# Attention and expert routing on one core: transposes of logits and early rows at the end of their slot, router constants in front

## The chip, the cores and the metric

The kernel runs on one core of one Trainium2 chip. The metric is the device time of one execution in microseconds. Five engines work from queues of their own, each in order, and wait for one another by semaphores: TensorE (PE in the profile; PEld is its weight load), VectorE (DVE), ScalarE (ACT), GpSimd (POOL) and SyncE (SP, which only issues transfers here).

## What is computed

```python
scores = scale * np.matmul(q, k.transpose(0, 1, 3, 2))        # q, k, v: 8 x 8 x 576 x 64
thresh = np.max(scores, axis=-1, keepdims=True) - tau
scores = np.where(scores >= thresh, scores, -1000000000.0)
attn = softmax(scores)                                        # sum + 1e-09 below
x = (attn @ v).transpose(0, 2, 1, 3).reshape(4608, 512)
logits = x @ w_gate                                           # 8 experts
# tokens go to experts greedily, by descending logit, at most 576 to an expert
for e in range(8): out[assigned == e] = np.maximum(x[assigned == e] @ w1[e], 0.0) @ w2[e]
```

## The kernel before

There are two stages. The first, `attention`, computes attention and logits for all 8 batches; the second, `moe`, chooses the tokens of each expert in turn (the class `Router` does that) and computes the experts. The change is in the first stage and in the constants that `Router` needs later.

A *pair* is two heads of one batch; there are 32 pairs, four to a batch. The scores of a pair are nine *tiles* of 128 rows by 576 keys: tiles 0 to 7 belong to one head each, tile 8 holds the last 64 rows of both heads ("a tile of two halves"). The work is written out by hand as a pipeline of *slots*, two tiles to a slot, 18 slots to a batch. The order of the program is the order in each engine's queue. In slot `s_` the loop does the following:

- `score` (L69, PE) computes the scores of two tiles into two PSUM tiles named `sc`. There are two such buffers in all, so the next slot's first scores need the first of them back and its second scores the second.
- `left` (L98, PE) turns the leftover columns of older tiles. It uses free columns of the last `sc` tile, from column HS = 288 on, in the two slots out of nine where a tile 8 is turned and the two after them (`p8` in the code).
- `beside`: in the other slots, one *side unit* if there is one, which also puts its results into the free columns of the `sc` tiles. Its PE part is issued here, behind the scores; its eviction `ev()` later on.
- `flush` (ACT) evicts finished outputs. `trev` (L116, L118, ACT) evicts the transposes `tb` of the slot before.
- `mx` (L74, DVE) copies the scores to `z` and reduces each row to its extreme; a threshold `nb` follows on POOL (L75). `ex` (L86, ACT) is the exponential of `z`. `leftev` (L128 to L131, ACT) evicts the leftovers.
- `stt` (L90, DVE) masks and sums the exponentials of the slot before, with the threshold of the slot before.
- `columns` issues *value units* (L155 and L165, PE): attention times v, taken from the list `queue` by due slots. Other entries of that list are run as they are reached: the reciprocals of a batch's sums (L170, L171, DVE), `finish`, and once, in the first batch, `Router.consts`. `whole` issues the logits of a finished batch (L177, PE), one half a slot.
- `tr` (L98, PE) turns two tiles of exponentials into `tb`, which has one buffer.

`finish(b)` puts the side units of batch b into the list `side`. `lgt_unit` turns the logits of the batch (ten transposes from `lt`, eight for one batch, and four small matmuls by `dup`, L185) into the free columns of both `sc` tiles; ACT evicts them (L217, L188, L219) and POOL scales and adds them (L222 to L229). It goes to the front of the list and becomes ready when the second half of the logits is evicted (L179). For the first two batches there are also ten units `xt_early`: each turns a quarter of the batch's attention output rows (four transposes from `xt`), ACT evicts it (L240), POOL copies the reciprocals (L239), and every second unit sends rows to DRAM.

`Router.consts` (L429 in the profile, since a wrapper records DVE's instructions) makes the router's constants on DVE from a table `cst` in SBUF, and two iotas on POOL.

The free slots of a batch, those without `p8`, are ten out of 18. Seen by their value work they come in three kinds: one whose second tile is a tile of two halves, one with eight matmuls L155 of 320 columns behind it, and one right after a slot of leftovers.

Of the kernel before, what the change touches and what calls it, by code (L numbers as in the profile page):

```python
# [22 lines left out]
def attention(ctx, tc, qk, vl, tau, wgd, xrows, xts, Lg, nb_batches, ident, dup, R, after_first):  # L23
# [28 lines left out]
        LD[p]=t  # L52


    SC={}; NBI={}; TH={}; PB={}; DEN={}
# [4 lines left out]
    def score(t):  # L60

        p,i=divmod(t,9); kd=LD[p]
        sc=ps_s.tile([128,2,512],F32,name="sc"); SC[t]=sc
        if i<8: todo=((i%2,slice(0,128),slice(i//2*128,i//2*128+128)),)
        else: todo=((0,slice(0,64),slice(512,576)),(1,slice(64,128),slice(512,576)))
        for h,o,c in todo:
            for f in range(2):
                r=slice(64*f,64*f+64)
                T.matmul(sc[o,f,:HS], kd["q",h][r,c], kd["k",h][r,:],start=True,stop=True)  # L69
# [97 lines left out]
    RD={}  # L167
# [13 lines left out]
    def free(t): return SC[t][:,:,HS:]  # L181
    def both(b,ps):
        for r in range(2):
            g=slice(64*r,64*r+64)
            T.matmul(ps[:,r,0:4],dup[g],RD[b][g,:,4,:,0],start=True,stop=True)  # L185
# [13 lines left out]
    def lgt_mm(b,c0,c1,ps):  # L199
        for c in range(c0,c1):  # L200
            a=HEAD(b)+128*c if c<2 else 128*c-256 if c<4 else 192 if b%2 and b<nb_batches-1 else 256
            turn(ps[:,:,64*(c-c0):64*(c-c0)+64],LT[b][:,a:a+128])
    def lgt_in(ps,n): return ps[:,:,0:64*n].rearrange("p r (m k) -> p r m k",k=32)[:,:,:,0:16]
    def logits(b,c0,c1,ps,o):
# [3 lines left out]
            V.tensor_tensor(w[:,:,:,r].rearrange("p c j h e -> p (c j) h e"),lv[:,r].rearrange("p m (h e) -> p m h e",h=2),  # L208
                RD[b][:,r,c0:c1].rearrange("p c j h -> p (c j) h").unsqueeze(3).to_broadcast([128,2*n,2,8]),op=ALU.mult)
        V.tensor_reduce(Lg[:,o:o+n,:],w.rearrange("p c j r h e -> p c e (j r h)"),axis=AX.X,op=ALU.add)  # L210
    def lgt_unit(b,ta,tb):
        n=5 if b<nb_batches-2 else 4
        x,y=free(ta),free(tb)
        lgt_mm(b,0,2,x); lgt_mm(b,2,n,y); both(b,x[:,:,128:])
        def ev():
            w=wk.tile([128,320],F32,name="lw",bufs=1).rearrange("p (r c j h e) -> p r c j h e",r=2,c=5,j=2,h=2)
            A.activation(w[:,:,0:2].rearrange("p r c j h e -> p r (c j) (h e)"),lgt_in(x,2),AF.Copy)  # L217
            both_ev(b,x[:,:,128:],slice(0,128),A)
            A.activation(w[:,:,2:n].rearrange("p r c j h e -> p r (c j) (h e)"),lgt_in(y,n-2),AF.Copy)  # L219
            for r in range(2):  # L220
                v=w[:,r,0:n].rearrange("p c j h e -> p (c j h) e")
                G.tensor_tensor(v,v,RD[b][:,r,0:n].rearrange("p c j h -> p (c j h)").unsqueeze(2).to_broadcast([128,4*n,8]),op=ALU.mult)  # L222
            v=w[:,:,0:n]
            G.tensor_tensor(v[:,0],v[:,0],v[:,1],op=ALU.add)
            G.tensor_tensor(v[:,0,:,0],v[:,0,:,0],v[:,0,:,1],op=ALU.add)
            G.tensor_tensor(Lg[:,4*b:4*b+4,:],v[:,0,0:4,0,0],v[:,0,0:4,0,1],op=ALU.add)
            if n==5:
                r=slice(64*(b%2),64*(b%2)+64)
                G.tensor_tensor(Lg[r,28+b//2,:],w[r,0,4,0,0],w[r,0,4,0,1],op=ALU.add)  # L229
        return ev  # L230
    XR={}
    def xt_early(b,c,i,t):
        n=128 if c<4 else 64
        y=free(t)
        for j in range(2): turn(y[:n,:,64*j:64*j+64],XT[b][:,2*i+j,c*128:c*128+n])
        if i==0: XR[b,c]=wk.tile([128,XW],F32,name="xr",bufs=XRB)
        xr=XR[b,c]
        def ev():
            if i==0: G.tensor_scalar(xr[:n,512:XW].rearrange("p (r k) -> p r k",r=2),RD[b][:n,:,c].rearrange("p r j h -> p r (j h)"),1.0,0.0,op0=ALU.mult,op1=ALU.add)  # L239
            A.activation(xr[:n,256*i:256*i+256].rearrange("p (j r d) -> p r j d",j=2,r=2),y[:n,:,0:128].rearrange("p r (j d) -> p r j d",j=2),AF.Copy)  # L240
            if i: nc.sync.dma_start(xrows[b*S+c*128:b*S+c*128+n,:],xr[:n])
        return ev
    def xt_unit(b,c,k=1):
        ps=bank_v([128,4,128],k)
        n=128 if c<4 else 64
# [25 lines left out]
        if j==3: queue.append(("n",lambda: not later,False,lambda: finish(b),p))  # L271
    def finish(b):
        aux.extend([lambda: lg_unit(b,0),lambda: lg_unit(b,1)])
        side.insert(0,(lambda: have.get("lt")==b,lambda *t: lgt_unit(b,*t)))
        rows=[lambda k=1,c=c: xt_unit(b,c,k) for c in range(5)]
        if nb_batches-NDEF-NBO<=b<nb_batches-NDEF:
            nc.sync.dma_start(xts[b],XT[b]); late2.extend(rows)
        elif b<nb_batches-NDEF: side.extend([(lambda: True,lambda ta,tb,c=c,i=i: xt_early(b,c,i,tb)) for c in range(5) for i in range(2)])
        else: late.extend(rows)
    def flush():  # L280
        for k,g in later: g(); k[0]=True
# [151 lines left out]
class Router:  # L433
    def __init__(s,ctx,tc,cst,off,Lg):
        nc=tc.nc; s.nc=nc; s.tc=tc
        s.V=Vec(nc.vector); s.A=nc.scalar; s.G=nc.gpsimd; s.T=nc.tensor
        s.cp=ctx.enter_context(tc.tile_pool(name="rcst",bufs=1))
        s.wk=ctx.enter_context(tc.tile_pool(name="rwk",bufs=2))
        s.L=Lg
        s.first=True; s.alone=True; s.pe=0.0; s.on=False; s.fill=lambda:None  # L440
        s.k=lambda n:cst[:,off[n][0]:off[n][0]+off[n][1]]
    def consts(s):
        V=s.V; G=s.G
        t=lambda n,sh,dt:s.cp.tile(sh,dt,name=n)
        s.ones=t("onesb",[128,128],BF16); V.memset(s.ones,1.0)
        s.tri=t("trib",[128,128],BF16); V.scalar_tensor_tensor(s.tri,s.k("eye"),BIGS,s.k("tri"),op0=ALU.mult,op1=ALU.add)
        s.eye=t("eyer",[128,128],F32R); V.tensor_copy(s.eye,s.k("eye"))
        s.gq=t("gq",[128,1+2*NC_],BF16); V.memset(s.gq[:,0:1],0.0)
        s.w8=t("w8b",[128,8],BF16); V.tensor_copy(s.w8,s.k("w8"))
        s.ihl=t("ihl",[128,2,NC_],BF16); V.tensor_copy(s.ihl[:,0],s.k("ihi")); V.tensor_copy(s.ihl[:,1],s.k("ilo"))  # L450

        s.e16=t("e16",[128,4,32],F32R); V.tensor_scalar(s.e16.rearrange("p c j -> p (c j)"),s.k("eye"),0.0,None,op0=ALU.mult)
        s.zz=t("zz",[128,4,224],BF16); V.memset(s.zz,0.0)
        for c in range(4):
            V.tensor_copy(s.e16[:,c,0:16],s.k("eye")[:,16*c:16*c+16])
            V.tensor_copy(s.zz[:,c,96:128],s.k("eye")[:,c:128:4])
        s.cmp=t("cmp",[128,NC_*J],BF16); s.fl=t("fla",[128,5],BF16); V.memset(s.fl,0.0)
# [556 lines left out]
```

## Time and profile before

| what | us |
|---|---|
| median of 3 timed runs (lowest, highest) | 981.51 (980.57, 982.38) |
| the profiled execution, and its span | 989.06, 987.3 |
| attention: first scores, last masking on DVE ends | 4.16, 445.1 |
| a batch, with early rows and without (87.49 to 144.06, 254.99 to 309.28) | 56.57, 54.29 |
| DVE reductions L74: 288, mean of one | 0.751 |
| DVE masking L90: 288, mean of one | 0.815 |
| ACT exponentials L86: 256 into `pp`, mean of one | 0.773 |

A timeline row has start, duration, engine, line, operation, output and input, and, where the engine stood idle before it, how long and for whom in brackets. Instructions of one kind that follow each other are merged, with their number behind an x. A matmul in float32 appears as two instructions for each one in the program, a transpose as one. Starts are recorded; the ends of matmuls are modelled.

### The profile page before, as it was taken

The page shows a single profiled execution, that of the slowest core. Times are in us where ns is not written, and L with a number is a line of the kernel's source. Part 1 is how long each engine was busy: PE and PEld are TensorE (multiplying, and loading weights), DVE is VectorE, ACT ScalarE, POOL GpSimd, SP SyncE. Part 2 cuts the span into 40 slices and gives each one's busy share as a digit, 9 for nine tenths or more (in the row PEclk, how much of TensorE's full clock was granted, in tenths as well). Part 3 has the DMA queues.
Part 4 walks back from the last instruction along what each step waited for, and adds up shares of the span by engine and source line. Part 5 has one row for each costly group of instructions (what it writes and reads, how often), then busy time and mean ns, then how long its engine had stood idle before and what let it go on. Part 6 is the DMA issues. An engine that isn't in the chain of part 4 may idle for free. (4 is left out here: it accounts for less than half of the span.)

```text
span 987.3 us, 24257 instructions
## 1 busy us (share of the span) xinstructions
PE 950.3 (96%) x9235; PEld 707.5 (72%) x9235; DVE 762.0 (77%) x2090; ACT 639.0 (65%) x1297; POOL 271.9 (28%) x454
## 2 busy tenths in 40 slices
PE   7999999999999999998789999999999999999996
PEld 4566656665566665565688797887978879898995
DVE  7999989999999999995688788686876786535220
ACT  6899999999999999996554354342542434545340
POOL 2334334343434343340100302122304022210202
PEclk9999999999999999999889999999999999999999
DMA  6230432632432333206732525251615234341101
GB/s 253 98 113 34 155 137 98 235 129 97 170 114 94 121 116 106 83 3 237 252 122 97 166 97 155 78 176 44 207 41 164 94 123 151 106 143 40 38 12 43
DMA packets 35860, 117.01 MB, mean 119 GB/s; under 512 B 4384, under 2 KB 5024, under 8 KB 35232
## 3 DMA queue, kind: packets, MB, share of 16 engines
q1 hardware_dynamic: 28352, 92.85, 27.3%
q0 software_dynamic: 5888, 19.03, 6.2%
q10 hardware_dynamic: 1504, 3.59, 1.2%
q8 instruction: 73, 1.20, 0.5%
q14 instruction: 43, 0.35, 0.1%
HBM read 93.01 MB, written 21.38 MB: 116 GB/s over the span
## 5 line engine op out<-in xcount | busy, mean ns | idle before, releaser
L74 DVE TENSOR_SCALAR_CACHE_REDUCE z<-sc 128x576 f32<-128x576 f32 x288 | 206.3, 751 | 22.2 <-PE sc L69 11.6
L86 ACT ACTIVATE pp<-z,nb 128x576 f32<-128x576 f32 x256 | 195.0, 773 | 32.4 <-DVE z L74 29.2
L75 POOL TENSOR_SCALAR nb<-nb,taub 128x1 f32<-128x1 f32 x288 | 140.0, 487 | 266.3 <-DVE z L74 201.9
L90 DVE SCALAR_TENSOR_TENSOR pp<-z,nb,pp 128x576 f32<-128x576 f32 x256 | 200.4, 815 | 0.0
L876 PE MATMUL pf<-w2h,H 128*128 128x512 f32 x576 | 194.9, 402 | 1.3 <-issue 0.6
L69 PE MATMUL sc<-qk 64*128 64x288 f32 (+1 forms) x1280 | 179.5, 424 | 3.6 <-DVE z L74 1.7
L155 PE MATMUL xo<-pt,vt 128*64 128x320 f32 (+1 forms) x1024 | 155.9, 420 | 0.0
L116 ACT ACTIVATE pt<-tb 128x512 f32<-128x512 f32 x253 | 137.7, 591 | 0.6
L883 POOL DMA_INDIRECT out_dram<-y,idx x40 | 43.7, 1092 | 323.8 <-ACT y L879 276.5
L876 PE MATMUL pf<-w2l,H 128*128 128x512 f32 x320 | 128.7, 402 | 0.0
L876 PEld LDWEIGHTS pf<-w2h,H 128*128 128x128 f32 x576 | 106.5, 188 | 22.1 <-issue 2.2
L98 PEld LDWEIGHTS tb<-ident,pp 64*128 64x128 f32 x2032 | 74.5, 138 | 61.6 <-issue 22.8
L69 PEld LDWEIGHTS sc<-qk 64*128 64x128 f32 (+1 forms) x1280 | 93.1, 178 | 32.9 <-DVE z L74 5.5
L844 PE MATMUL pf<-xh,w1h 128*128 128x288 f32 (+2 forms) x512 | 110.6, 302 | 0.7 <-ACT xh L790 0.7
L844 PE MATMUL pf<-xl,w1h 128*128 128x288 f32 (+2 forms) x512 | 111.0, 303 | 0.0
L844 PE MATMUL pf<-xh,w1l 128*128 128x288 f32 (+2 forms) x512 | 110.4, 301 | 0.3 <-issue 0.3
L879 ACT ACTIVATE y<-pf 128x512 f32<-128x512 f32 x40 | 23.9, 598 | 130.4 <-PE pf L876 127.3
L856 ACT ACTIVATE hf<-pf 128x576 f32<-128x576 f32 x56 | 36.5, 652 | 95.7 <-PE pf L844 83.6
L155 PEld LDWEIGHTS xo<-pt,vt 128*64 128x64 f32 x1024 | 60.6, 136 | 52.6 <-issue 25.5
L98 PE MATMUL tb<-ident,pp 64*128 64x64 f32 x2032 | 93.3, 229 | 3.3 <-ACT pt L116 3.0
L844 PEld LDWEIGHTS pf<-xh,w1h 128*128 128x128 f32 x512 | 82.7, 191 | 1.6 <-ACT xh L790 1.1
L844 PEld LDWEIGHTS pf<-xh,w1l 128*128 128x128 f32 x512 | 82.3, 190 | 0.6 <-issue 0.5
(198 smaller groups left out, 1331.5 us busy)
## 6 DMA issues: line engine op xcount, KB each, us to landing
qk<-qk_dram SPq DMA_DIRECT2D x31, 864.0 KB, 4.7
vt<-vl_dram SPq DMA_DIRECT2D x32, 576.0 KB, 6.6
w2s<-w_dram SPq DMA_DIRECT2D x32, 512.0 KB, 5.9
w1s<-w_dram SPq DMA_DIRECT2D x28, 512.0 KB, 6.3
xrows<-pp SPq DMA_DIRECT2D x24, 260.0 KB, 2.6
xts<-xt SPq DMA_DIRECT2D x2, 1152.0 KB
pt<-xts SPq DMA_DIRECT2D x2, 1152.0 KB, 5.1
xrows<-xr SPq DMA_DIRECT2D x8, 260.0 KB
```

The source lines that it names most:

```text
L69: T.matmul(sc[o,f,:HS], kd["q",h][r,c], kd["k",h][r,:],start=True,stop=True)
L74: V.tensor_scalar(z,SC.pop(t)[:,:,:HS],-0.125,None,op0=ALU.mult,op1=ALU.min,accum_out=nb[:,0:1])
L75: G.tensor_scalar(nb[:,1:2],nb[:,0:1],taub[:,0:1],None,op0=ALU.add)
L86: A.activation(pview(t),ZB[t].rearrange("p a b -> p (a b)"),AF.Exp,bias=NBI[t][:,0:1],scale=-1.0)
L90: V.scalar_tensor_tensor(pv,ZB.pop(t).rearrange("p a b -> p (a b)"),NBI[t][:,1:2],pv,op0=ALU.is_le,op1=ALU.mult,accum_out=den_of(p)[:,p%4/ ...
L98: g=slice(64*r,64*r+64); T.transpose(o[:,r],x[r%len(x)][g],ident[g,g])
L116: else: A.activation(o,tb,AF.Copy)
L155: T.matmul(xo[64*h:64*h+64,:q.stop-q.start],v[:,f,128*u+64*h:128*u+64*h+64],PT[p][:,h,u,q],start=new,stop=last,skip_group_check=True)
L844: T.matmul(ps[:,h,:n],s[w][:,k,f*128:(f+1)*128],s[x][:,k,cols[h]],start=(i==0),stop=(i==11))
L856: A.activation(hf,ps[:,:,:HS],AF.Relu)
L876: T.matmul(ps[:,0,:],H[:,f,c:c+128],s[w][:,f],start=(f==0 and j==0),stop=e)
L883: G.indirect_dma_start(out=out,out_offset=IOA(ap=s["idx"][:n,t:t+1],axis=0),in_=y[:n],in_offset=None)
```

## The change

Three things change. The side units are taken at the end of the slot, behind `columns` and `whole` and ahead of `tr`; they use the last `sc` tile of the slot only, and their evictions follow directly, behind both exponentials. The logits' unit is cut into two units for two slots: chunks 0 to 2, then the rest with the small matmuls. And the router's constants that can be made from the identity matrix are made by a new function, `setup`, before the first slot; of the rest, one stays on DVE and three small conversions and a memset go to POOL. In the changed file the side units read `FREE`, a second record of the `sc` tiles, since `mx` has removed the tile from `SC` by then.

```diff
-    def lgt_unit(b,ta,tb):
+    LW={}
+    def lgt_unit(b,half,t):
         n=5 if b<nb_batches-2 else 4
-        x,y=free(ta),free(tb)
-        lgt_mm(b,0,2,x); lgt_mm(b,2,n,y); both(b,x[:,:,128:])
-        def ev():
...
+        c0,c1=((0,3),(3,n))[half]; y=free(t)
+        lgt_mm(b,c0,c1,y)
+        if half: both(b,y[:,:,128:])
+        else: LW[b]=wk.tile([128,320],F32,name="lw",bufs=1).rearrange("p (r c j h e) -> p r c j h e",r=2,c=5,j=2,h=2)
+        w=LW[b]
+        A.activation(w[:,:,c0:c1].rearrange("p r c j h e -> p r (c j) (h e)"),lgt_in(y,c1-c0),AF.Copy)
+        if half: both_ev(b,y[:,:,128:],slice(0,128),A)
+        for r in range(2):
+            v=w[:,r,c0:c1].rearrange("p c j h e -> p (c j h) e")
+            G.tensor_tensor(v,v,RD[b][:,r,c0:c1].rearrange("p c j h -> p (c j h)").unsqueeze(2).to_broadcast([128,4*(c1-c0),8]),op=ALU.mult)
...
-        side.insert(0,(lambda: have.get("lt")==b,lambda *t: lgt_unit(b,*t)))
+        side[:0]=[(lambda: have.get("lt")==b,lambda t,i=i: lgt_unit(b,i,t)) for i in range(2)]
...
     after_first()
+    R.setup(ident)
...
         for p,n in p8: left(p,n,SC[sc_[-1]])
-        ready=[] if p8 else [x for x in side if x[0]()]
-        if ready: side.remove(ready[0])
-        beside=ready[0][1](*sc_) if ready else None
...
         for t in sc_[:1]: ex(t)
         for p,n in p8: leftev(p,n)
-        if beside: beside()
         for t in sc_[1:]: ex(t)
...
         if sc_: columns(); whole()
+        ready=[x for x in side if x[0]()]
+        if ready and not p8: side.remove(ready[0]); ready[0][1](sc_[-1])
         for t in tr_: tr(t,t==tr_[0])
...
+    def setup(s,ident):
+        V=s.V
+        t=lambda n,sh,dt:s.cp.tile(sh,dt,name=n)
+        s.ones=t("onesb",[128,128],BF16); V.memset(s.ones,1.0)
+        s.eye=t("eyer",[128,128],F32R); V.tensor_copy(s.eye,ident)
+        s.gq=t("gq",[128,1+2*NC_],BF16); V.memset(s.gq[:,0:1],0.0)
+        s.e16=t("e16",[128,4,32],F32R); V.tensor_scalar(s.e16.rearrange("p c j -> p (c j)"),ident,0.0,None,op0=ALU.mult)
+        s.zz=t("zz",[128,4,224],BF16); V.memset(s.zz,0.0)
+        for c in range(4):
+            V.tensor_copy(s.e16[:,c,0:16],ident[:,16*c:16*c+16])
+            V.tensor_copy(s.zz[:,c,96:128],ident[:,c:128:4])
     def consts(s):
...
         s.tri=t("trib",[128,128],BF16); V.scalar_tensor_tensor(s.tri,s.k("eye"),BIGS,s.k("tri"),op0=ALU.mult,op1=ALU.add)
...
+        s.w8=t("w8b",[128,8],BF16); G.tensor_scalar(s.w8,s.k("w8"),1.0,0.0,op0=ALU.mult,op1=ALU.add)
+        s.ihl=t("ihl",[128,2,NC_],BF16)
+        for i,n in enumerate(("ihi","ilo")): G.tensor_scalar(s.ihl[:,i],s.k(n),1.0,0.0,op0=ALU.mult,op1=ALU.add)
+        s.cmp=t("cmp",[128,NC_*J],BF16); s.fl=t("fla",[128,5],BF16); G.memset(s.fl,0.0)
```

`xt_early` changes in the same way: its eviction is no longer put off into a function, and stands directly behind its transposes.

How the queues change is seen best at the first logits. In PE's queue before, two slots of the second batch, from the scores of one to the end of the other (`sc` scores or free columns, `xo` value outputs, `xt` attention output, `lt` logits, `tb` transposed exponentials; a number behind x counts equal instructions):

```order
L69 MATMUL sc<-qk 64x288 x4
L98 MATMUL sc<-ident,xt 128x64 x4
L165 MATMUL xo_1272<-pl,vt 64x256 x2
L165 MATMUL xo_1393<-pl,vt 64x320 x2
L155 MATMUL xo_1393<-pt,vt 64x320 x2
L98 MATMUL tb<-ident,pp 128x64 x16
L69 MATMUL sc<-qk 128x288 x4
L98 MATMUL sc<-ident,lt 128x64 x10
L185 MATMUL sc<-rd,dup 128x4 x2
L155 MATMUL xo_1393<-pt,vt 64x320 x4
L98 MATMUL tb<-ident,pp 128x64 x16
```

The same two slots in the changed kernel:

```order
L69 MATMUL sc<-qk 64x288 x4
L165 MATMUL xo_1272<-pl,vt 64x256 x2
L165 MATMUL xo_1386<-pl,vt 64x320 x2
L155 MATMUL xo_1386<-pt,vt 64x320 x2
L98 MATMUL sc<-ident,lt 128x64 x6
L98 MATMUL tb<-ident,pp 128x64 x16
L69 MATMUL sc<-qk 128x288 x4
L155 MATMUL xo_1386<-pt,vt 64x320 x4
L98 MATMUL sc<-ident,lt 128x64 x4
L185 MATMUL sc<-rd,dup 128x4 x2
L98 MATMUL tb<-ident,pp 128x64 x16
```

The logits' ten transposes stood between scores and value units of one slot; they are now six and four, behind the value units of two slots. The first is one slot earlier than before and takes the place of an early-rows unit, which comes later.

ACT's queue before, in the same two slots, from the first slot's first exponential to the second slot's last one:

```order
L86 ACTIVATE pp<-z,nb 128x576
L240 ACTIVATE xr<-sc 128x2x2x64
L86 ACTIVATE pm_101<-z,nb 128x576
L145 ACTIVATE xt<-xo_1272 128x256
L116 ACTIVATE pt<-tb 128x2x4x64 x2
L86 ACTIVATE pp<-z,nb 128x576
L217 ACTIVATE lw<-sc 128x2x64
L188 ACTIVATE rd<-sc 128x2x2x2
L219 ACTIVATE lw<-sc 128x2x96
L86 ACTIVATE pp<-z,nb 128x576
```

And in the changed kernel, up to the evictions that now follow that exponential:

```order
L86 ACTIVATE pp<-z,nb 128x576
L86 ACTIVATE pm_101<-z,nb 128x576
L219 ACTIVATE lw<-sc 128x2x96
L145 ACTIVATE xt<-xo_1272 128x256
L116 ACTIVATE pt<-tb 128x2x4x64 x2
L86 ACTIVATE pp<-z,nb 128x576 x2
L219 ACTIVATE lw<-sc 128x2x64
L188 ACTIVATE rd<-sc 128x2x2x2
```

The evictions of the side units have gone from between the two exponentials of a slot to behind both.

The constants: POOL's queue in the changed kernel, at the place in the first batch where only the three last of these rows stood between thresholds before.

```order
L75 TENSOR_SCALAR nb<-nb,taub 128x1 x18
L454 TENSOR_SCALAR w8b<-cst 128x8
L456 TENSOR_SCALAR ihl<-cst 128x36 x2
L457 MEMSET fla 128x5
L459 IOTA pio 128x128
L460 TENSOR_SCALAR pio<-pio 128x128
L462 IOTA pih 128x720
```

Three conversions and a memset have come ahead of the iotas. On DVE, 13 instructions of `setup` stand behind the memset of `idle` and ahead of the first reduction, and `trib` alone is left at the old place.

More of the change, by code (lines that the diff above doesn't have):

```diff
@@ L52, in load @@
         LD[p]=t
-    SC={}; NBI={}; TH={}; PB={}; DEN={}
+    SC={}; FREE={}; NBI={}; TH={}; PB={}; DEN={}
     def den_of(p):
@@ L62, in score @@
         p,i=divmod(t,9); kd=LD[p]
-        sc=ps_s.tile([128,2,512],F32,name="sc"); SC[t]=sc
+        sc=ps_s.tile([128,2,512],F32,name="sc"); SC[t]=sc; FREE[t]=sc
         if i<8: todo=((i%2,slice(0,128),slice(i//2*128,i//2*128+128)),)
@@ L180, in HEAD, with free @@
     def HEAD(b): return S-256+(D if b==nb_batches-1 else 0)
-    def free(t): return SC[t][:,:,HS:]
+    def free(t): return FREE[t][:,:,HS:]
     def both(b,ps):
@@ L210, in logits @@
         V.tensor_reduce(Lg[:,o:o+n,:],w.rearrange("p c j r h e -> p c e (j r h)"),axis=AX.X,op=ALU.add)
-    def lgt_unit(b,ta,tb):
+    LW={}
+    def lgt_unit(b,half,t):
         n=5 if b<nb_batches-2 else 4
-        x,y=free(ta),free(tb)
-        lgt_mm(b,0,2,x); lgt_mm(b,2,n,y); both(b,x[:,:,128:])
-        def ev():
[L216 to L230, printed above, removed]
@@ L231, in attention @@
+        v=w[:,:,c0:c1]
+        G.tensor_tensor(v[:,0],v[:,0],v[:,1],op=ALU.add)
+        G.tensor_tensor(v[:,0,:,0],v[:,0,:,0],v[:,0,:,1],op=ALU.add)
+        m=min(c1,4)-c0
+        G.tensor_tensor(Lg[:,4*b+c0:4*b+c0+m,:],v[:,0,0:m,0,0],v[:,0,0:m,0,1],op=ALU.add)
+        if c1==5:
+            r=slice(64*(b%2),64*(b%2)+64)
+            G.tensor_tensor(Lg[r,28+b//2,:],w[r,0,4,0,0],w[r,0,4,0,1],op=ALU.add)
     XR={}
@@ L237, in xt_early @@
         xr=XR[b,c]
[L238 to L242, printed above, removed]
+        if i==0: G.tensor_scalar(xr[:n,512:XW].rearrange("p (r k) -> p r k",r=2),RD[b][:n,:,c].rearrange("p r j h -> p r (j h)"),1.0,0.0,op0=ALU.mult,op1=ALU.add)
+        A.activation(xr[:n,256*i:256*i+256].rearrange("p (j r d) -> p r j d",j=2,r=2),y[:n,:,0:128].rearrange("p r (j d) -> p r j d",j=2),AF.Copy)
+        if i: nc.sync.dma_start(xrows[b*S+c*128:b*S+c*128+n,:],xr[:n])
     def xt_unit(b,c,k=1):
@@ L277, in finish @@
             nc.sync.dma_start(xts[b],XT[b]); late2.extend(rows)
-        elif b<nb_batches-NDEF: side.extend([(lambda: True,lambda ta,tb,c=c,i=i: xt_early(b,c,i,tb)) for c in range(5) for i in range(2)])
+        elif b<nb_batches-NDEF: side.extend([(lambda: True,lambda t,c=c,i=i: xt_early(b,c,i,t)) for c in range(5) for i in range(2)])
         else: late.extend(rows)
@@ L444, in consts @@
         t=lambda n,sh,dt:s.cp.tile(sh,dt,name=n)
-        s.ones=t("onesb",[128,128],BF16); V.memset(s.ones,1.0)
         s.tri=t("trib",[128,128],BF16); V.scalar_tensor_tensor(s.tri,s.k("eye"),BIGS,s.k("tri"),op0=ALU.mult,op1=ALU.add)
[L447 to L457, printed above, removed]
+        s.w8=t("w8b",[128,8],BF16); G.tensor_scalar(s.w8,s.k("w8"),1.0,0.0,op0=ALU.mult,op1=ALU.add)
+        s.ihl=t("ihl",[128,2,NC_],BF16)
+        for i,n in enumerate(("ihi","ilo")): G.tensor_scalar(s.ihl[:,i],s.k(n),1.0,0.0,op0=ALU.mult,op1=ALU.add)
+        s.cmp=t("cmp",[128,NC_*J],BF16); s.fl=t("fla",[128,5],BF16); G.memset(s.fl,0.0)
         pi=t("pio",[128,32,4],BF16); s.pio=pi
```

## Prediction

> **What bounds the kernel now.** I read first the busy times by stretch, with the attention stage cut where the logits of one batch give way to the next. Columns: the stretch, its length, then each engine's busy time with its instructions.
>
> ```profile
> core 0: us, PE busy (x) PEld busy (x) DVE busy (x) ACT busy (x) POOL busy (x), PEclk, DMA share, GB/s
> 144.06:200.66 56.60, 56.56 (x716) 34.70 (x718) 52.74 (x147) 53.29 (x110) 24.24 (x48) 1.00 0.47 171
> 200.66:254.99 54.33, 54.29 (x684) 33.08 (x686) 52.25 (x147) 50.96 (x102) 20.98 (x43) 1.00 0.42 148
> ```
>
> A batch takes 56.60 us while early rows are turned (ten units in it) and 54.33 us when they are not. PE is idle for 0.04 us of either, DVE for 3.9 and 2.1 us. A busy PE alone proves little, since the ends of matmuls are modelled, so I also compared starts: the rows below show that one kind of PE work takes the same time from its own start to the next one's, wherever it stands (16 transposes 0.55 us, for example). PE sets the pace here; DVE and ACT follow with 4 to 7% to spare. Next the waits, between 30 and 440 us:
>
> ```profile
> DVE z L74 <- PE sc L185: 8.2, 7, 1.3
> DVE z L74 <- PE sc L69: 7.4, 18, 0.6
> PEld sc L69 <- ACT rd L188: 1.3, 7, 0.2
> ```
>
> DVE stands longest for the logits' transposes, 8.2 us in seven places. That looks like the prize, but PE is at work in those times. What PE itself loses there is the last row, 0.2 us in each place. So the sum goes by what PE does and waits for, not by DVE's idle time.
>
> **Logits' transposes, seven times.** One of the places, before:
>
> ```profile
> 85.77 1.19 PE L69 MATMUL sc<-qk 64*128 64x288 f32 x8
> 86.80 0.47 PE L98 MATMUL sc<-ident,lt 64*128 64x64 f32 x10
> 87.10 0.34 PE L185 MATMUL sc<-rd,dup 64*128 64x4 f32 x4
> 87.37 1.30 PE L155 MATMUL xo<-pt,vt 128*64 128x320 f32 x8
> 87.49 0.76 DVE L74 TENSOR_SCALAR_CACHE_REDUCE z<-sc 128x576 f32<-128x576 f32 x1 [1.30 <-PE sc L185]
> 88.60 0.71 PE L98 MATMUL tb<-ident,pp 64*128 64x64 f32 x16
> 89.35 1.24 PE L69 MATMUL sc<-qk 64*128 64x288 f32 x8
> ```
>
> and slots of the same two kinds, first with early rows and then, late in the stage, with nothing beside:
>
> ```profile
> 110.31 1.35 PE L69 MATMUL sc<-qk 64*128 64x288 f32 x12
> ...
> 111.59 0.34 PE L98 MATMUL sc<-ident,xt 64*128 64x64 f32 x4
> ...
> 113.24 0.71 PE L98 MATMUL tb<-ident,pp 64*128 64x64 f32 x16
> ...
> 113.79 1.19 PE L69 MATMUL sc<-qk 64*128 64x288 f32 x8
> ...
> 116.26 0.71 PE L98 MATMUL tb<-ident,pp 64*128 64x64 f32 x16
> ```
>
> ```profile
> 385.72 1.35 PE L69 MATMUL sc<-qk 64*128 64x288 f32 x12
> ...
> 388.22 0.71 PE L98 MATMUL tb<-ident,pp 64*128 64x64 f32 x16
> 388.76 1.19 PE L69 MATMUL sc<-qk 64*128 64x288 f32 x8
> ...
> 391.11 0.71 PE L98 MATMUL tb<-ident,pp 64*128 64x64 f32 x16
> ```
>
> From scores to the slot's own transposes PE takes 2.35 us bare (388.76 to 391.11) and 2.83 us with the logits (85.77 to 88.60): 0.48 us. Then the next scores come 0.75 us after those transposes (88.60 to 89.35) where 0.55 is normal (113.24 to 113.79), because the buffer's eviction on ACT ends late: 0.20 us. Together 0.68 us. Afterwards the ten transposes stand directly ahead of 16 of their own kind, which take 0.55/16 = 0.034 us each: 0.34 us for both parts, and the four small matmuls 0.27 us (87.10 to 87.37): 0.61 us. The late eviction goes if ACT keeps up (below). 7 x 0.07 = **0.5 us saved**; from 0.6 us lost, if those 0.20 us stay and the split costs 0.1 us more at places with slack of their own, to 1.5 us saved.
>
> **Early rows, twenty units.** They cost 56.60 - 54.33 = 2.27 us a batch, 4.5 us in two batches: 0.43 us in a slot with a tile of two halves (113.24 - 110.31 = 2.93 against 2.50) and 0.12 us in the other (2.47 against 2.35). The row at 111.59 shows why: standing between scores and value units, four transposes add a change of matmul shape, and behind the 12-part scores a longer one. Moved ahead of the slot's 16 transposes they should cost 4 x 0.034 = 0.14 us, 2.8 us in all: **1.7 us saved**, bounded by 0 (they cost there what they did here) and 3.
>
> **New waits, the price of the move.** The unit now writes a score tile that DVE may still be reading, and is evicted behind both exponentials; the second scores of the next slot need that eviction. In the slot at 113.79:
>
> ```profile
> 115.23 0.75 DVE L74 TENSOR_SCALAR_CACHE_REDUCE z<-sc 128x576 f32<-128x576 f32 x1
> ...
> 116.03 0.38 ACT L240 ACTIVATE xr<-sc 128x256 f32<-128x256 f32 x1
> ```
>
> DVE is done with the last tile at 115.98; PE would arrive at 113.79 + 2.35 = 116.14: 0.1 us to spare. On ACT the second exponential goes into the row at 116.03, so the eviction ends by 116.03 + 0.77 + 0.38 = 117.2; the second scores come at 116.14 + 0.14 + 0.55 + 0.5 = 117.3. Both fit, barely. They don't fit in two other kinds of slot:
>
> ```profile
> 95.18 1.24 PE L69 MATMUL sc<-qk 64*128 64x288 f32 x8
> ...
> 96.77 0.75 DVE L74 TENSOR_SCALAR_CACHE_REDUCE z<-sc 128x576 f32<-128x576 f32 x1
> ...
> 97.14 0.77 ACT L86 ACTIVATE pp<-z,nb 128x576 f32<-128x576 f32 x1
> ...
> 97.59 0.71 PE L98 MATMUL tb<-ident,pp 64*128 64x64 f32 x16
> ```
>
> ```profile
> 125.49 1.35 PE L69 MATMUL sc<-qk 64*128 64x288 f32 x12
> ...
> 127.36 0.75 DVE L74 TENSOR_SCALAR_CACHE_REDUCE z<-sc 128x576 f32<-128x576 f32 x1
> ```
>
> The first comes right behind the slots that evict leftovers, and ACT starts late: first exponential 97.14, second by 97.91, eviction done by 98.68 + 0.38 = 99.06, while PE wants the buffer at 97.59 - 0.12 + 0.14 + 0.55 + 0.5 = 98.66. That is 0.4 us at most, less where ACT overlaps its instructions; I take 0.2 us in five such slots (two a batch; with two of a batch's ten free slots given to logits, the twenty units spread over two and a half batches). In the second kind DVE made the reciprocals first: last tile done 128.11, PE there at 125.49 + 2.50 = 127.99; 0.1 to 0.2 us, in two batches. Sum **1.4 us lost**, between 0.3 us (all but the second kind hidden) and 6 us (0.2 us in nearly all of the 34 units).
>
> PSUM — Partial Sum Buffer of the Trainium skill, in its section "PSUM bank collisions raise a hardware error", says that engines must be kept apart by bank, not by address. By that rule the moved transposes wait for DVE's read of the whole tile though they write other columns. The trace agrees from the other side: at 87.49 DVE waited 1.30 us for matmuls into columns that it does not read.
>
> **Constants.** They stand in DVE's queue between two slots:
>
> ```profile
> 36.26 0.17 DVE L429 MEMSET onesb<- 128x128 bf16 x1
> ...
> 37.66 0.71 PE L98 MATMUL tb<-ident,pp 64*128 64x64 f32 x16
> ...
> 38.70 0.75 DVE L74 TENSOR_SCALAR_CACHE_REDUCE z<-sc 128x576 f32<-128x576 f32 x1
> ...
> 39.51 0.76 PE L69 MATMUL sc<-qk 64*128 64x288 f32 x4 [1.14 <-DVE z L74]
> ...
> 40.96 0.76 PE L69 MATMUL sc<-qk 64*128 64x288 f32 x4 [0.69 <-ACT pl L131]
> ```
>
> DVE loses 38.70 - 36.26 = 2.4 us, less 0.1 us for the one instruction that stays. PE loses 39.51 - 37.66 - 0.55 = 1.30 us ahead of the first scores and 1.45 - 0.52 = 0.93 us ahead of the second: **2.2 us saved**, bounded by 1.3 and 2.4. In front they go where DVE stands idle anyway:
>
> ```profile
> 1.96 0.11 DVE L334 MEMSET idle<- 128x64 uint32 x1
> ...
> 5.54 0.76 DVE L74 TENSOR_SCALAR_CACHE_REDUCE z<-sc 128x576 f32<-128x576 f32 x1 [3.46 <-PE sc L69]
> ```
>
> The 13 instructions need under 2.4 us of those 3.46, behind the tile that PE's first matmuls wait for; if that cover were short, the start would slip by the rest. Three small operations move to POOL, priced by the nearest:
>
> ```profile
> L239 POOL TENSOR_SCALAR xr<-rd 128x8 f32<-128x8 f32 (+1 forms) x10 | 6.8, 678 | 0.0
> ```
>
> 3 x 0.68 = 2.0 us ahead of the iotas. Behind them in POOL's queue are the thresholds, which DVE needs a slot later, 2.8 us: I cost it at nothing, at most 0.7 us.
>
> **Sum.** 0.5 + 1.7 - 1.4 + 2.2 = 3.0 us, hence 989.06 - 3.0 = 986.1 for the profiled execution. That one is 7.5 us above the median of the timed runs; the stage is the same in both, so I take the difference over: 981.5 - 3.0 = **978.5 us**.
>
> **Rivals.**
> *DVE is the bound.* Then its 8.2 us of stalls and the constants' 2.3 go: 971.0 us. For it: DVE waits in just these places. Against: PE's 0.04 us. Perfetto Trace Analysis of the Trainium skill, section "Identifying the Most-Contended Engine", would read it so: matmul busy is no good measure of PE's headroom, LDWEIGHTS busy is, here 34.70/56.60 = 61% against DVE's 93%. The constant start-to-start times speak against that reading. Chance 0.06.
> *ACT becomes the bound, slower.* If evictions behind the second exponential come 0.3 us late in all 34 units, 10.2 us go and 4.4 come back: 987.3 us. It decides from 4.4/34 = 0.13 us a unit. For: margins of 0.1 us, ACT at 94%. Against: the sums of the slot at 113.79. Chance 0.08.
> *Only the constants count.* The moved units cost behind what they cost before: 979.3 us. Chance 0.18.
> *Not even those.* POOL's longer queue, or PE work that was merely late, gives the 2.2 us back within two slots: 981.5 us. Chance 0.08.
>
> **Numbers.** My forecast has 0.60, by itself 976.8 to 980.2 us. The range 975.8 to 980.9 takes in the constants alone and leaves out the first two rivals and the last one's middle. A measurement here tells about 0.2%, 2 us, from no change: below 979.5 counts as faster. Faster: 0.54 of the forecast, 0.06 and 0.12 from the first and third rival, 0.72. Same: 0.06 + 0.06 + 0.07 = 0.19. Slower 0.09.
>
> **What would show it.** Right: PE without a gap from 30 to 440 us; stretches of about 54.3 us without early rows and 56.4 with them (0.9 us less for the units, 0.7 us of new waits); no row of 2.4 us of constants near 36; DVE no longer waiting for L185. Wrong: scores that wait for the evictions of lw, rd or xr on ACT, or transposes of lt and xt that wait for DVE's reduction, in most slots instead of some seven; or DVE's first reduction later than 5.54 us.

## The result, and the profile after

The changed kernel takes 973.83 us (median of 6 runs, 972.87 to 975.12), the kernel before 981.28 us (6 runs, 979.90 to 984.98): ratio 0.9919, 95% interval 0.9901 to 0.9938. That is 7.45 us, where 3.0 were forecast, and lies below the forecast's range. The profiled execution took 973.59 us, its span 971.8 us.

The windows of the changed kernel, cut again where the last small matmuls of a batch's logits start; the first stretch has eight units of early rows in it, the second four:

```profile
core 0: us, PE busy (x) PEld busy (x) DVE busy (x) ACT busy (x) POOL busy (x), PEclk, DMA share, GB/s
141.66:196.85 55.19, 55.12 (x714) 33.57 (x714) 52.64 (x147) 52.86 (x110) 24.57 (x53) 1.00 0.42 147
196.85:251.36 54.51, 54.51 (x700) 33.13 (x698) 52.47 (x147) 51.96 (x106) 22.64 (x51) 1.00 0.41 140
```

PE still has no gap worth the name, and the first stretch took 55.19 us where 56.4 was forecast (for ten units; two of the free slots now hold logits). The waits of the changed kernel between 30 and 440 us (engine, line, what it waited for; sum, times, longest):

```profile
PEld sc L98 <- DVE z L74: 17.2, 34, 0.6
DVE z L74 <- PE sc L69: 11.7, 34, 0.6
PEld sc L69 <- ACT xr L240: 2.2, 7, 0.4
```

The 8.2 us in which DVE waited for line 185 are gone. In all 34 moved units the weight load now waits for DVE's reduction (as PSUM — Partial Sum Buffer of the Trainium skill, "PSUM bank collisions raise a hardware error", would have it, by bank and not by address). By the letter this is one of the forecast's signs of being wrong: waits for DVE's reduction in most slots. But a load's idle time counts from the load before it, and PE is at work in most of it. The groups by line below show what reaches PE itself (last column: idle time just before).

```profile
L98 PE MATMUL sc<-ident,xt 64*128 64x64 f32 (+1 forms) x80 | 6.6, 244 | 0.1
L98 PE MATMUL sc<-ident,lt 64*128 64x64 f32 x68 | 5.1, 243 | 0.0
```

By the modelled ends PE waits 0.1 us ahead of the moved transposes, in all; by the starts it is 0.14 us in each of two slots, shown below under the failed step. The two slots in which one batch's logits now stand, PE's timeline:

```profile
82.47 0.76 PE L155 MATMUL xo<-pt,vt 128*64 128x320 f32 x4
83.16 0.40 PE L98 MATMUL sc<-ident,lt 64*128 64x64 f32 x6
83.40 0.66 PE L98 MATMUL tb<-ident,pp 64*128 64x64 f32 x16
83.90 1.19 PE L69 MATMUL sc<-qk 64*128 64x288 f32 x8
85.01 1.30 PE L155 MATMUL xo<-pt,vt 128*64 128x320 f32 x8
86.24 0.34 PE L98 MATMUL sc<-ident,lt 64*128 64x64 f32 x4
86.42 0.34 PE L185 MATMUL sc<-rd,dup 64*128 64x4 f32 x4
86.61 0.69 PE L98 MATMUL tb<-ident,pp 64*128 64x64 f32 x16
87.14 1.19 PE L69 MATMUL sc<-qk 64*128 64x288 f32 x8
```

Six transposes take 0.24 us to the next start, four 0.18, the four small matmuls 0.19, and the slot's own 16 then need 0.50 and 0.53 instead of 0.55: the unit costs 0.24 + 0.18 + 0.19 - 0.07 = 0.54 us, against 0.68 before and 0.61 in the forecast. The place of the constants, all engines but ACT and the loads, and the start of DVE's queue:

```profile
1.96 0.11 DVE L333 MEMSET idle<- 128x64 uint32 x1
...
3.47 0.18 DVE L426 CAST zz<-ident 128x32 bf16<-128x32 f32 x1
5.54 0.76 DVE L74 TENSOR_SCALAR_CACHE_REDUCE z<-sc 128x576 f32<-128x576 f32 x1 [1.88 <-PE sc L69]
```

```profile
36.32 0.68 POOL L454 TENSOR_SCALAR w8b<-cst 128x8 bf16<-128x8 f32 x1
...
36.87 0.28 DVE L426 SCALAR_TENSOR_TENSOR trib<-cst 128x128 bf16<-128x128 f32 x1
36.97 0.44 POOL L456 TENSOR_SCALAR ihl<-cst 128x36 bf16<-128x36 f32 x2
37.07 0.74 DVE L74 TENSOR_SCALAR_CACHE_REDUCE z<-sc 128x576 f32<-128x576 f32 x1
```

In front the 13 instructions end by 3.65 us and the first reduction starts at 5.54 us, as before. Between the slots DVE does 0.20 us (36.87 to 37.07) instead of 2.4.

Two things make the totals hard to read. The first masking comes at 9.1 to 10.3 us, whichever the kernel, so I measure attention from the first masking (L90) to the start of the last one; below this is called the masking time. Each is read from one profiled execution. And nothing that the diff says touches the expert stage, yet its instructions stand in another order: behind the last masking they are the same instructions, but 940 of 3825 instructions on PE, 237 of 902 instructions on DVE and 46 of 484 on ACT stand at another place in the queue. The wrapper that records DVE's operations also counts a planner's clock, 0.125 us and a part by size for each; four small operations that moved to POOL are no longer counted, the clock stands 0.59 us lower, and the planner of the expert stage, which places router steps by that clock, decides otherwise in places.

### The profile page after: what moved, and what is told of

Its sections match the earlier page's. It is cut to its first block, busy times and chain, and to the rows that moved or that the text cites. A ratio compares the mean times of both kernels' runs of the same rounds, so it can differ in the third digit from the quotient of the medians.

```text
span 971.8 us, 24280 instructions
## 1 busy us (share of the span) xinstructions
PE 943.4 (97%) x9235; PEld 704.5 (72%) x9235; DVE 764.0 (79%) x2086; ACT 639.3 (66%) x1297; POOL 279.8 (29%) x493
## 4 chain that ended last, share of the span: by engine, by line
PE 89%; DVE 5%; DMA 3%; issue 2%; ACT 1%; POOLq 0%; SPq 0%; ACTq 0%; DVEq 0%
PE pf L844 22%; PE pf L876 20%; PE sc L69 15%; PE xo L155 14%; PE tb L98 8%; PE sc L98 2%; PE pt L789 2%; PE xo L165 2%; DVE pp L90 1%; PE rps L497 1%; DVE z L74 1%; DVE cmp L426 1%; PE xo L177 1%; PE xo L246 1%; DMA out_dram<-y,idx 1%
## 5 line engine op out<-in xcount | busy, mean ns | idle before, releaser
L75 POOL TENSOR_SCALAR nb<-nb,taub 128x1 f32<-128x1 f32 x288 | 144.9, 504 | 249.9 <-DVE z L74 187.3
L90 DVE SCALAR_TENSOR_TENSOR pp<-z,nb,pp 128x576 f32<-128x576 f32 x256 | 200.0, 813 | 0.0
```

The source lines that it names most:

```text
L75: G.tensor_scalar(nb[:,1:2],nb[:,0:1],taub[:,0:1],None,op0=ALU.add)
L90: V.scalar_tensor_tensor(pv,ZB.pop(t).rearrange("p a b -> p (a b)"),NBI[t][:,1:2],pv,op0=ALU.is_le,op1=ALU.mult,accum_out=den_of(p)[:,p%4/ ...
```

## Experiments

The first set takes the change apart.

**The changed kernel, expert stage in the order of before.**

```diff
-    R.setup(ident)
+    R.setup(ident); R.V.free+=0.125*4+(8+36+36+5)/0.96/1000
```

> The changed kernel, but the planner's clock for DVE starts as far on as it did before, so that the expert stage is issued in the order of before. Theory A (the moves save about 6 us in attention, the new order of the expert stage another 1.5): 975.3 us, ratio to before 0.994, and 1 to 2 us slower than the changed kernel. Theory B (the order of the expert stage is worth nothing; all of the 7.45 us is in attention or the router): 973.8 us, ratio 0.992. In the trace the last masking of attention is near 439 us in both.

974.16 us (973.91 to 974.95, 5 runs), ratio 0.9923 (0.9904 to 0.9941). In the trace every instruction behind the last masking stands where it stood before. The masking time is 428.77 us, in the changed kernel 428.78, in the kernel before 435.10. Attention gains 6.3 us, whatever the expert stage's order. By the medians, which come from two sets of runs, the new order gives 0.3 us: nearer to theory B than to A.

**The kernel before, expert stage in the order of after.**

```diff
     s.cmp=t("cmp",[128,NC_*J],BF16)
+    s.V.free-=0.125*4+(8+36+36+5)/0.96/1000
```

> The kernel before, with the planner's clock set back so that the expert stage is issued in the changed kernel's order; attention as before. Theory A: 1 to 2 us faster than before, ratio 0.9985. Theory B: the same as before, ratio 1.000. Last masking at 445 us in both.

980.81 us (979.17 to 982.84, 11 runs), 1.2 us below the kernel before in the same set (981.98, 22 runs); ratio 0.9985 (0.9970 to 0.9999): theory A's figure. So the order is worth 0.3 to 1.2 us by the two pairs of medians, and neither settles the size. From the last masking to the end of the span the order of after took 532.3 and 533.2 us (this kernel, the changed one), that of before 533.9 to 535.5 in the six others of this set and the next whose granted clock was 0.990 or 0.991, which agrees with some 1 us. (These clocks are means of the whole span.)

The masking time of this kernel was 436.57 us, 1.5 us more than that of the kernel before, though its attention stage was left as it was. The last section shows where: the granted clock fell to half for 3.4 us. So a masking time can be off by 1.5 us for that reason; without such a fall, those of equal attention stages agree within 0.1 us (435.10 and 435.04, 428.78 and 428.77).

**Constants alone, and the moves alone**, both with the old order of experts. The first has `setup` and `consts` of the change in the kernel before; the second has `consts` of before in the changed kernel.

```diff
     after_first()
+    R.setup(ident); R.V.free+=0.125*4+(8+36+36+5)/0.96/1000
```

> Only the constants moved (setup in front, three conversions and a memset on POOL); transposes and the order of the expert stage as before. Theory A: 2.3 us faster, ratio 0.9977, masking behind the constants 2.3 us earlier. Theory B (PE-bound slots give it back later, or POOL's longer queue holds DVE up): ratio 0.999 to 1.000, the lead of 2.3 us gone by the end of attention.

```diff
     after_first()
-    R.setup(ident)
```

> Only the transposes moved and the logits split; constants in DVE's queue at the old place, expert stage in the order of before. Theory A: 4.0 us saved in attention (2.0 by the logits, 2.0 by the early rows, no new waits), ratio 0.996. Theory B (the constants' place decides, the transposes only change places): 0.5 to 1 us, ratio 0.999.

Constants: 979.96 us (977.51 to 980.79, 11 runs), ratio 0.9971 (0.9957 to 0.9985); masking time 432.79 us, 2.31 saved. Moves: 976.70 us (975.87 to 978.85, 6 runs), ratio 0.9949 (0.9932 to 0.9966); 431.07 us, 4.03 saved. 2.31 + 4.03 = 6.34 is what both give together. The constants' lead is there 400 us later, so nothing gave it back. By the masking time theory A holds in both.

**Each move alone**, with the constants in front: the changed kernel, in which a second list holds the units that go back behind the scores, in their old form. First the early rows go back, then the logits.

```diff
-side.extend([(lambda: True,lambda t,c=c,i=i: xt_early(b,c,i,t)) for c in range(5) for i in range(2)])
+side2.extend([(lambda: True,lambda ta,tb,c=c,i=i: xt_early(b,c,i,tb)) for c in range(5) for i in range(2)])
...
         for p,n in p8: left(p,n,SC[sc_[-1]])
+        ready=[] if p8 or not sc_ else [x for x in side2 if x[0]()]
+        if any(x[0]() for x in side): ready=[]
+        if ready: side2.remove(ready[0])
+        beside=ready[0][1](*sc_) if ready else None
```

> The changed kernel with the early rows put back behind the scores; the logits stay in two parts at the end of the slot, the constants in front, and the expert stage in the order of before. The two moves saved 4.03 us together; the batches without early rows tell how it divides: 0.26 us a batch for the logits (54.28 to 54.02), 1.8 us in seven, and the other 2.2 us in the twenty units of early rows. A (the moves don't touch each other): the masking of the last tile starts at 442.1 - 1.8 = 440.3 us; time 2.2 us above the changed kernel in this order, some 976.3. B (as on record, 0.5 us for the logits): the masking at 441.6, time some 977.7. C (the logits give their share only where rows have left the slot behind the scores free): the masking above 441.6.

```diff
-side[:0]=[(lambda: have.get("lt")==b,lambda t,i=i: lgt_unit(b,i,t)) for i in range(2)]
+side2.insert(0,(lambda: have.get("lt")==b,lambda *t: lgt_unit(b,*t)))
```

> The other half: early rows at the end of the slot, the logits whole and behind the scores as before; constants in front, expert stage in the order of before. A: the masking of the last tile starts at 442.1 - 2.2 = 439.9 us, time 1.8 us above the changed kernel in this order, some 976.0. B (as on record, 1.7 us for the rows and up to 1.4 us of new waits against it): between 440.4 and 441.8, time 976.5 to 977.9. With the run before it the sum of the two halves is tested: 442.1 less both savings must be 438.0.

Logits: 977.19 us (976.47 to 977.42), ratio 0.9952 (0.9934 to 0.9969); masking time 431.15 us, that is 432.79 - 431.15 = 1.64 saved. Rows: 976.48 us (975.78 to 977.19), ratio 0.9948 (0.9931 to 0.9965); 430.74 us, 2.05 saved. The two give 3.69 of 4.02 us; the other 0.33 comes only with both, in the batches that have both. By the last masking (440.4 and 440.0 us) A holds in both runs. By the median of the logits' run alone, 977.19 us, one couldn't tell A (976.3) from B (977.7).

**Logits whole, on both score tiles, at the slot's end.**

```diff
-side[:0]=[(lambda: have.get("lt")==b,lambda t,i=i: lgt_unit(b,i,t)) for i in range(2)]
+side.insert(0,(lambda: have.get("lt")==b,lambda t: (lgt_unit(b,0,t-1),lgt_unit(b,1,t))))
```

> The changed kernel with the logits of a batch turned whole, in one slot, over both score tiles, at the slot's end; rows and constants as in the changed kernel, expert stage in the order of before. Is the cut into two parts needed? A (the end of the slot is what counts): 10 transposes at 0.034 us and the four small matmuls at 0.18 us are what the two parts cost together, 0.5 us; ACT has three evictions, 0.33 + 0.17 + 0.27 us, where one had a margin of 0.43 to 0.58 us ahead of the second scores; the first scores need the first tile, which is evicted first. So up to 0.3 us of wait in seven slots: the masking of the last tile starts between 438.0 and 440.0 us. B (the cut carries the gain): 0.3 to 0.6 us a batch lost, the masking at 440 to 442 us.

Masking time 428.70 us against 428.77 with the cut; 975.46 us (973.88 to 976.19, 6 runs), ratio 0.9935 (0.9919 to 0.9951). The median is 1.3 us above the 974.16 with the cut, from another set of runs; the two profiled executions took 973.88 and 973.91 us. In attention the cut into two parts carries nothing; the place does.

**Every eviction of a moved unit twice**, here that of the rows; the copy into `lw` likewise.

```diff
         A.activation(xr[:n,256*i:256*i+256].rearrange("p (j r d) -> p r j d",j=2,r=2),y[:n,:,0:128].rearrange("p r (j d) -> p r j d",j=2),AF.Copy)
+        A.activation(xr[:n,256*i:256*i+256].rearrange("p (j r d) -> p r j d",j=2,r=2),y[:n,:,0:128].rearrange("p r (j d) -> p r j d",j=2),AF.Copy)
```

> The changed kernel (expert stage in the order of before) with every eviction of a moved unit on ACT made twice, so that the score tile comes free 0.25 to 0.37 us later in 34 slots. A (the margins read from the changed kernel's trace, from the end of the eviction to the second scores: 0.4 to 0.6 us in 14 slots of logits, 0.25 to 0.3 us in 11 slots of rows, under 0.2 us in seven): 1 to 3 us lost, the masking of the last tile at 439 to 441 us. B (the margin of 0.1 us on record, in all slots): 34 x 0.2 = 7 us lost, the masking at 445 us. C (ACT is never waited for there): no change, 438.0 us.

Masking time 433.73 us, 5.0 us lost; 980.99 us (980.12 to 982.96, 12 runs). Between A and B. The batches without early rows lose 0.1 us each, so nearly all of it falls on the twenty units of rows, 0.23 us each. Two successive slots of that kernel:

```profile
183.60 0.36 ACT L241 ACTIVATE xr<-sc 128x256 f32<-128x256 f32 x1
184.00 0.38 ACT L242 ACTIVATE xr<-sc 128x256 f32<-128x256 f32 x1
```

```profile
183.76 1.43 PE L69 MATMUL sc<-qk 64*128 64x288 f32 x8
185.12 1.30 PE L155 MATMUL xo<-pt,vt 128*64 128x320 f32 x8
```

The second eviction ends 0.42 us after the first (184.38 against 183.96), and from scores to value units PE needs 1.36 us instead of 1.11 (83.90 to 85.01 above): 0.25 lost. Not all of that is the wait. The trace's single rows have the second scores start at 184.43, 0.05 us behind the eviction, which is 0.68 us after the first scores where 0.54 is normal: 0.14 us late. The matmul behind the wait then takes 0.35 us to the next start instead of 0.24. So the margin in this slot was 0.42 - 0.14 = 0.28 us.

In the changed kernel itself no second scores wait for the eviction. They start 0.19 to 0.44 us after its end in fifteen slots of rows, 0.09 to 0.17 in the five ahead of a slot with a tile of two halves, and 0.44 to 0.53 in the fourteen of logits; 0.05 of that is the least that the waiting ones above need. The margin of 0.1 us on record was right for those five slots and too small elsewhere. In the run with doubled evictions the second scores wait in all twenty units of rows and in none of the logits'.

Of the last set there is one execution each, and every program in it, the kernel before (993.37 us) included, was 9 to 15 us longer, all of it in the expert stage; so these are read by the attention stage alone.

**More work on TensorE, and more on VectorE.**

```diff
-        for j in range(2): turn(y[:n,:,64*j:64*j+64],XT[b][:,2*i+j,c*128:c*128+n])
+        for j in (0,1,0,1): turn(y[:n,:,64*j:64*j+64],XT[b][:,2*i+j,c*128:c*128+n])
```

> Is TensorE or VectorE the bound of the attention stage? The changed kernel (expert stage in the order of before), with the four transposes of each of the twenty early-row units done twice: work on TensorE alone, 4 x 0.034 = 0.14 us a unit. A (TensorE sets the pace): 20 x 0.14 = 2.7 us lost, the masking of the last tile starts at 440.7 us instead of 438.0; up to 0.5 us more where the eviction behind the unit, 0.14 us later too, has no margin. B (VectorE sets it): 438.0 us.

```diff
         for j in range(2): turn(y[:n,:,64*j:64*j+64],XT[b][:,2*i+j,c*128:c*128+n])
+        V.memset(dmy,0.0)
```

> The counterpart: one memset of 128x128 bf16 more on VectorE (0.17 us for the like in the profile of before) beside each of the twenty early-row units, ahead of the next slot's reductions. A (TensorE sets the pace, VectorE has some 0.14 us of idle time in such a slot): at most 0.5 us lost, the masking of the last tile between 438.0 and 438.5 us. B (VectorE sets it): 20 x 0.17 = 3.4 us lost, 441.4 us.

```profile
L237 DVE MEMSET dmy<- 128x64 uint32 x20 | 2.2, 112 | 0.0
```

With 80 transposes more on PE the masking time is 430.98 us, 2.2 lost: 0.11 us a unit. With 2.2 us more on DVE (the row above: twenty of 0.112 us, not the 0.17 I had expected) it is 428.94 us, 0.17 lost: a tenth of a microsecond a unit fits into DVE's idle time. TensorE sets the pace, VectorE doesn't. By the rule of the Trainium skill (Perfetto Trace Analysis, "Identifying the Most-Contended Engine"), the loads' 33.57 us in a stretch of 55.19, 61%, would still clear TensorE; these two runs decide against it here.

**Units behind the slot's own transposes.**

```diff
+        for t in tr_: tr(t,t==tr_[0])
         ready=[x for x in side if x[0]()]
         if ready and not p8: side.remove(ready[0]); ready[0][1](sc_[-1])
-        for t in tr_: tr(t,t==tr_[0])
```

> The changed kernel (expert stage in the order of before) with the moved units directly behind the slot's own 16 transposes instead of ahead of them: the same matmuls next to the same neighbours in shape, but the eviction comes 0.55 us later against the next scores. A (what saves time is the neighbour, what limits it is the eviction, whose margin is 0.1 us in most slots of rows and 0.3 to 0.45 us in those of logits): the eviction, 0.37 us, ends some 0.2 us after the second scores could start, 0.2 us in 34 slots; the masking of the last tile starts at 442 to 445 us instead of 438.0. B (the place in the slot's end doesn't matter): 438.0 us. C (a unit behind the transposes delays the next scores by itself, without the eviction): 438.0 plus 0.05 to 0.1 us in 34 slots, 440 to 441 us, and no wait for ACT ahead of the second scores.

Masking time 434.40 us, 5.6 us lost, A's range (4 to 7). One slot:

```profile
182.52 0.71 PE L98 MATMUL tb<-ident,pp 64*128 64x64 f32 x16
183.07 0.29 PE L98 MATMUL sc<-ident,xt 64*128 64x64 f32 x4
183.19 1.53 PE L69 MATMUL sc<-qk 64*128 64x288 f32 x8
183.53 0.38 ACT L240 ACTIVATE xr<-sc 128x256 f32<-128x256 f32 x1
184.65 1.30 PE L155 MATMUL xo<-pt,vt 128*64 128x320 f32 x8
```

The four transposes cost 0.12 us here, no more than ahead. The second scores could have begun at 183.19 + 0.54 = 183.73, but the eviction ends at 183.91 and they begin 0.05 us behind it, 0.24 late; the matmuls behind the wait lose another 0.1 as above, so scores to value units take 1.46 us instead of 1.11. The neighbour is as good on this side, the eviction isn't.

**The kernel before, once more.**

> The kernel before once more, unchanged, for a second profile of it: that of the forecast had a span of 987.3 us, and its expert stage took 489.4 us where the changed kernel's took 480.4. A (those 9 us are one execution's): the stretch from the end of attention (line 115's last row) to the end of the span is 529 to 533 us, as in the other profiles, and not 539.6; the masking of the last tile starts at 444.3 +/- 0.3 us, so a span of 977 to 981. B (the expert stage of before is slower by itself): 536 us or more, a span of 984 or more.

Masking time 435.04 us, as in the first profile (435.10). From line 115's last row to the end of the span it took 541.0 us: the number is B's. From the last masking that stretch is 544.4 us; the three variants of the changed kernel beside it took 542.8 to 548.8, where their like took 532 to 537 in the other sets. A slow expert stage is therefore no property of the kernel before; nor is it one execution's, as A had it.

## Why the prediction was wrong

Right: that PE bounds the attention stage, and that DVE's 8.2 us of waits were no prize (2.2 us more on DVE cost 0.17); that the constants would be hidden in front, 2.31 us for 2.2; that POOL's longer queue costs nothing; that most moved units would find DVE's reduction just done.

**The step that failed first: "New waits, the price of the move", 1.4 us.** It was mis-sized: some 0.3 us of it is there, and none of that comes from an eviction. (Early rows fell into three slots of the first kind, not five.) The first of its two kinds of slot, right behind the evictions of leftovers, in the changed kernel:

```profile
92.92 1.19 PE L69 MATMUL sc<-qk 64*128 64x288 f32 x8
...
94.70 1.43 ACT L86 ACTIVATE pp<-z,nb 128x576 f32<-128x576 f32 x2
...
95.87 1.35 PE L69 MATMUL sc<-qk 64*128 64x288 f32 x12
96.03 0.37 ACT L240 ACTIVATE xr<-sc 128x256 f32<-128x256 f32 x1
...
97.04 0.71 PE L165 MATMUL xo<-pl,vt 64*64 64x256 f32 x8
```

The forecast had the eviction end 99.06 - 95.18 = 3.88 us after the slot's scores start, since it took the first exponential from the profile of before, 1.96 us after the scores, and added durations. Here the first exponential comes at 94.70 - 92.92 = 1.78 us and the pair takes 1.43 us, not 1.54; the eviction starts 0.10 us before the pair ends and ends at 96.40, 3.48 us after the scores. Of the 0.40 us by which that is earlier, 0.18 are the exponential's, and 0.22 are overlap on ACT that the sum of durations left out. The scores behind it take 1.17 us to the next unit, as bare ones do. The second kind, behind the reciprocals, came as forecast, 0.14 us in each of two slots: from value units to the moved transposes it is 0.83 us here, where 0.69 is normal (82.47 to 83.16 above).

```profile
124.47 0.76 PE L155 MATMUL xo<-pt,vt 128*64 128x320 f32 x4
125.30 0.34 PE L98 MATMUL sc<-ident,xt 64*128 64x64 f32 x4
```

The late exponential of the first kind was the old logits' own doing, as two bare slots of the same kind in the profile of before show, the first far from any logits, the second three slots behind them:

```profile
343.15 1.19 PE L69 MATMUL sc<-qk 64*128 64x288 f32 x8
...
344.94 1.44 ACT L86 ACTIVATE pp<-z,nb 128x576 f32<-128x576 f32 x2
```

```profile
371.25 1.25 PE L69 MATMUL sc<-qk 64*128 64x288 f32 x8
...
373.22 1.44 ACT L86 ACTIVATE pp<-z,nb 128x576 f32<-128x576 f32 x2
```

1.79 us from scores to exponentials in the first, 1.97 in the second, where the scores themselves take 0.06 us longer. The run with the early rows alone, whose logits still stand behind the scores, confirms it. The slot of the first kind there:

```profile
92.60 1.24 PE L69 MATMUL sc<-qk 64*128 64x288 f32 x8
...
94.55 1.44 ACT L86 ACTIVATE pp<-z,nb 128x576 f32<-128x576 f32 x2
...
95.01 0.34 PE L98 MATMUL sc<-ident,xt 64*128 64x64 f32 x4
...
95.89 0.37 ACT L240 ACTIVATE xr<-sc 128x256 f32<-128x256 f32 x1
```

The exponential is late again, 1.95 us after the scores; with the logits alone moved it comes at 1.79. So I had read a delay that the change removes as one that stays. Even with it the next second scores aren't held up by the eviction: they start 0.63 us after the first ones, as in bare slots of their kind. What waits there is the moved unit, for DVE's reduction: 2.41 us from the scores to it instead of 2.28 (92.92 to 95.20 in the changed kernel).

The margin was thin, but not everywhere as thin as I said: 0.42 us more on ACT cost 0.23 us a unit of rows, and units placed 0.55 us later lost 5.6 us. The rival with ACT as the bound was near: evictions that end some 0.4 us later took back 5.0 us, more than the 4.0 that the moves had given.

**"Logits' transposes", 0.5 us**, were worth 1.64 alone: also mis-sized. 7 x (0.68 - 0.54) = 1.0 us stands in the slot itself. The rest stands in the slots that follow, such as that at 371.25, which I had priced only to the next scores. The run with the logits moved, against the one with the constants alone, gives it slot by slot in a batch without early rows: 0.14 us in the slots of the logits, 0.05 in the one right behind them, 0.06 in the third behind. The whole is 54.29 us before and 54.03 after from masking to masking, 0.26 us a batch. **"Early rows", 1.7 us**, gave 2.05 alone with their waits in; the doubled transposes show a unit's own cost, 0.11 us for the 0.14 taken. Another 0.33 us comes only with both moves: the three slots of the first kind take 3.09, 3.09 and 3.05 us in the run with the rows alone and 2.96, 2.92 and 2.96 in the changed kernel, where the logits' delay is gone.

So attention: 1.64 + 2.05 + 0.33 + 2.31 = 6.3 us, against 0.5 + 1.7 - 1.4 + 2.2 = 3.0. A part of what stays to 7.45 us is the **planner's clock**, which the forecast missed: 0.3 to 1.2 us by the runs. I had looked at the order of instructions only in the stage that the diff names. But medians hold something else too: with the old order the changed kernel's was 7.8 us below before in its set (974.16 against 981.98), 1.5 more than attention explains. That goes with TensorE's granted clock, which is listed for each run. Eleven of the 22 executions of before had 0.990 or 0.991 and a median of 980.5 us, 6.3 above 974.16, whose five executions had the same; the other eleven had 0.986 to 0.989 and took 981.9 to 985.2 us. How much of the 7.45 us is the order and how much the clock isn't settled.

The forecast took over its 3.0 us from the profile of before, an execution 7.5 us longer than the median, because "the stage is the same in both". The excess was in the expert stage: 543.0 us from the last masking to the end, where the same order took 533.9 to 536.6 in the first two sets. So that subtraction was sound.

## What to carry to other kernels

Where an engine has no gap, price a small step by its neighbours' shapes: four transposes cost 0.11 to 0.13 us beside their like and 0.12 to 0.43 us elsewhere, and what may limit the better place is when its buffer is emptied, which a doubled eviction measures directly. When forecasting a wait, ask whether the lateness seen in the old profile was made by the very step that moves. Where a planner counts the operations that it issues, compare the order of the whole program, not of the stage that was edited.

## What the runs showed of the hardware

In the four profiles of the last set, and in the first one of before, PE, DVE and ACT stop together at places in the expert stage, three to five times, 3.2 to 5.5 us in all; eight of the nine profiles of the other sets have no such stop over 0.3 us, one has a single one of 1.1 us. One of them, from the run with the added memset:

```profile
760.57 0.19 DVE L427 CAST cn<-rps 128x32 fp32r<-128x32 f32 x1 [2.98 <-remote]
760.61 0.65 ACT L857 ACTIVATE hf<-pf 128x576 f32<-128x576 f32 x1 [3.52 <-remote]
...
760.81 0.29 PE L504 MATMUL rps<-cn,e 128*32 128x8 f32 x4 [2.22 <-DVE cn L427]
```

What the engines wait for isn't recorded ("remote").

The granted clock falls to half for 3.4 us or a multiple of it, at two or more places of every profile. Once it did so in attention, in the kernel before with the expert stage in the order of after (columns as in the windows above; the clock is the third number from the end):

```profile
41.80:45.20 3.40, 3.19 (x12) 1.27 (x12) 3.36 (x11) 3.17 (x6) 1.26 (x3) 0.50 0.01 2
```

```profile
42.01 1.33 PE L69 MATMUL sc<-qk 64*128 64x288 f32 x4 [0.69 <-ACT pl L131]
...
43.27 2.14 PE L155 MATMUL xo<-pt,vt 128*64 128x256 f32 x8
```

The same matmuls take 0.76 and 1.19 us in the first profile of before, at 40.96 and 41.64, and the attention stage of this execution came out 1.5 us longer. In front of the fall PE had stood still for 1.14 us, for DVE's constants. In the 14 profiles every half-clock stretch ahead of the end of the program begins within 5 us of the start of a pause of PE of over 1.1 us. But not every such pause is followed by one: the same pause in the first profile of before isn't. So that the pause brings it is likely, not shown.

The stops and the clock go together in the same way: behind the stop at about 760 us, four of the five profiles that have it show 3.4 us at half clock, and no other profile shows any there. What brings the stops stays open.
